# Projection of a linear-attention kernel: four fp32 tiles of 64x64 in place of three fp32r products with zero-padded weights

## The chip, the cores and the metric

The kernel runs on one core of a Trainium2 chip. The metric is the device time of one execution in microseconds (us); where several runs were made, their median. TensorE (PE in the profile) multiplies, VectorE (DVE), ScalarE (ACT) and GpSimd (POOL) work on tiles in on-chip memory (SBUF) and on the eight accumulation banks (PSUM, 2 KB per partition each), and SyncE (SP) issues nearly all transfers.

## The reference

Eight batches of eight heads of 576 tokens with 64 numbers each are put through linear attention; the result goes through a top-1 mixture of experts (MoE).

```python
def phi(x):
    proj = np.einsum('bhsd,df->bhsf', x, w_phi)                       # 64 -> 128
    proj = proj - np.max(np.abs(proj), axis=-1, keepdims=True)
    return np.concatenate([np.exp(proj), np.exp(-proj)], axis=-1)     # 256
q_p, k_p = phi(q), phi(k)
kv = np.einsum('bhsf,bhsd->bhfd', k_p, v)
z = np.sum(k_p, axis=2)
num = np.einsum('bhsf,bhfd->bhsd', q_p, kv)
den = np.einsum('bhsf,bhf->bhs', q_p, z)[..., None] + 1e-06
x = num / den        # then [4608, 512] for the experts
...
# MoE: tokens with x @ w_skip > 0 go to their best of 8 experts (512 -> 1024 -> 512)
out[do_compute] = xc + gate * (relu(xc @ w1[e]) @ w2[e])
```

The change is in the first line of phi, for q and for k.

## The kernel before

**Units and steps.** The attention works on *units*: four heads of one batch, of k or of q. There are 16 k units and 16 q units, two of each per batch. A unit has five items: item 0 is the tail (64 tokens of each head pair), items 1 to 4 are the main part (a head pair and 256 tokens each). Both streams advance by one item per step; the q stream runs 6 steps behind the k stream (`off` in CFG), so one batch of k and of q takes ten steps. Within a step the stages have lags (`lag` in CFG): load, transpose, projection one step later, exponentials at 3, use at 4, the z row at 5 and kva at 6.

**Load** (`st_load`, L251 to L259). The raw numbers of a unit lie in a tile `raw` of [128 partitions, 2 head pairs, 18 tokens, 32 numbers]; a partition is (half of the 64 numbers, head of the pair, run of 18 tokens). SP issues four DMAs per unit at L256, each to 64 partitions, 144 KB in runs of 128 bytes. Four buffers serve both streams. The load of the next unit of a stream is asked for at item 0 of the unit before it, but its buffer is free only when VectorE has made the last transpose out of it. SP works its queue in order; on it also stand the loads of v (L265, L274), the stores of `xrows` (L503, L505, L564, L566) and of `out` (L630, L635). Each DMA is bound to one of eight completion semaphores in turn, and the program makes it wait until the DMA that used that semaphore eight places earlier has landed.

**Transpose** (`st_t`, L276 to L296). VectorE transposes 32x32 blocks: the tail into `xTt` at L289, half a unit into `xT` at L291. After that a column of xT is a pair of tokens of two heads. ScalarE rounds it to fp32r (`hi`, L292), and the rest `lo` = xT - hi is made at L294, by GpSimd but for six early ones, which VectorE makes (`ini` in CFG).

**Projection** (`st_proj`, L298 to L326). Per block of 128 columns three fp32r matmuls with 256 result columns add up hi times wph, hi times wpl and lo times wph (L306 to L308). wph and wpl are the two parts of w_phi, padded with zeros so that either half of the result columns belongs to one head of the pair (`setup_w`). The result fills one PSUM bank, tag P; VectorE takes the row maximum of the absolute values (L312) and subtracts it into `u` (L321).

**Exponentials and use.** For k, ScalarE makes exp(u) and exp(-u) at L344 and L345, GpSimd sums rows for z (L353 to L359), TensorE multiplies with v (L388, L395), and z is summed in four 32-column tiles (L406). For q, TensorE transposes u into a bank U (L366), ScalarE makes the exponentials (L372, L373), TensorE multiplies with kva (L486), and VectorE divides by den in `norm` (L437 to L449). At the end of a batch `post` (L513 on) picks each token's expert on VectorE with small instructions (L538 to L561), and its stores go out through SP.

**What sets the order.** On TensorE the order of steps 8 to 78 is written out by hand; elsewhere a scheduler orders each engine's instructions by what it expects of the times, and the order is fixed before the program runs. PSUM is one pool for attention and MoE: K one bank, P three, U two, O two. The experts follow from L756 on; they load weights, round them to fp32r in parts (L188, L189) and multiply.

Of the kernel before, what the change touches and what calls it, by code (L numbers as in the profile page):

```python
# [20 lines left out]
CFG = {'ql': -2, 'q1': 0, 'vtl': 3, 'at': 6, 'cp': 0, 'ini': 'vvpvppvvpvp', 'inz': '', 'lo': {('E', 0): 'pppvpppp', ('E', 1): 'pppppppp'}, 'lod': 'vppvvvpv', 'seq': ('E', 'E', 'C', 'C', 'SC', 'D', 'DS', 'C', 'C', 'D'), 'pre': (2,), 'rows': (1, 2), 'rxg': (0,) * 6, 'lag': (1, 3, 4, 5, 6), 'post': (4, 5, 7), 'hook': (-1, -1, -1), 'man': (8, 79), 'dnow': 0, 'off': 6, 'order': 'EPAZUT', 'direct': (), 'nb': {'K': 1, 'P': 3, 'U': 2, 'O': 2}, 'apools': (('ld', 2), ('hl', 5), ('up', 5), ('zp', 2), ('ep', 7), ('kvp', 6), ('xp', 2)), 'mpools': (('rawp', 1), ('mx', 2), ('mo', 2), ('wseta', 1), ('wsetb', 1))}  # L21
# [3 lines left out]
def kernel(  # L25
# [27 lines left out]
    # a row of xrows: the token, its gate, its number  # L53
# [3 lines left out]
    # slots: full ones, ones of up to 192 tokens, ones of up to 128  # L57
# [9 lines left out]
    ps = ctx.enter_context(tc.tile_pool(name="ps", bufs=2, space=PSUM))  # L67
    NB = CFG["nb"]
    DIRECT = CFG["direct"]

    xrows = dram.tile([NTOK, XW], F32, name="xrows")

    def bank(tag):
        return ps.tile([P, 512], F32, tag=tag, name="ps_" + tag, bufs=NB[tag])
# [7 lines left out]
    # w_phi in the rows of either head of a pair, and which rows are whose  # L82
    wsrc = const.tile([P, NF], F32, name="wsrc")
    own = const.tile([P, 2], F32, name="own")
    nc.vector.memset(own, 0.0)
    for dh in range(2):
        for hd in range(2):
            nc.vector.memset(own[dh * 64 + hd * 32:dh * 64 + hd * 32 + 32, hd:hd + 1], 1.0)
    wph = const.tile([P, 2 * NF], F32R, name="wph")
    wpl = const.tile([P, 2 * NF], F32R, name="wpl")  # L90

    def setup_w():
        for hd in range(2):
            c = slice(hd * NF, (hd + 1) * NF)
            nc.scalar.activation(out=wph[:, c], in_=wsrc, func=AF.Copy, scale=own[:, hd:hd + 1])
            nc.vector.scalar_tensor_tensor(
                out=wpl[:, c], in0=wsrc, scalar=own[:, hd:hd + 1], in1=wph[:, c].bitcast(F32),
                op0=ALU.mult, op1=ALU.subtract)
# [8 lines left out]
    # the tails of a quad's v, each pair in its own rows, zeros in the other's  # L107
# [16 lines left out]
    # of every slot: the rows to gather and the rows to scatter to  # L124
# [85 lines left out]
    def places(g, pad, v):  # L210
        # v is 0 in an empty place, else 1 + the row to gather; what to add so that no row is scattered from an empty one
        nc.vector.tensor_scalar(out=g, in0=v, scalar1=-1.0, scalar2=0.0, op0=ALU.add, op1=ALU.max)
        nc.vector.tensor_scalar(out=pad, in0=v, scalar1=0.0, scalar2=BIG, op0=ALU.is_equal, op1=ALU.mult)

    early = []
    # ------------------------------------------------------------------ attention
    with ExitStack() as actx:
        pools = {}
        for nm, bufs in CFG["apools"]:
# [3 lines left out]
        # a head is 32 runs of 18 tokens; partition (half of d, head of the pair, run)  # L223
# [6 lines left out]
        # rows of xrows: two batches after each other, then the tails of both  # L230
# [8 lines left out]
        for b in range(B):  # L239
            for kind in ("k", "q"):  # L240
                for hq in range(NQ):
                    u = Unit()
                    u.kind, u.b, u.hq, u.g = kind, b, hq, b * NQ + hq
                    u.u, u.e, u.z, u.hlp = {}, {}, {}, {}
# [6 lines left out]
        def st_load(u):  # L251
            src = kv_in[u.kind]
            u.raw = ld.tile([P, 2, 18, 32], F32, tag="raw", name="raw", bufs=4)
            for pr in range(2):
                for dh in range(2):
                    nc.sync.dma_start(  # L256
                        out=u.raw[dh * 64:dh * 64 + 64, pr],
# [466 lines left out]
        for t in range(n + OFF + LA):  # L724
# [26 lines left out]
            if t == 0:  # L751
                setup_w()
# [382 lines left out]
```

## Time and profile before

| | before |
|---|---|
| time, median of 3 runs (lowest to highest) | 683.41 us (681.26 to 686.98) |
| span of the profiled execution | 681.4 us |
| attention, from the start to the last product with kva | about 390 us |
| busy: PE / DVE / ACT / POOL | 600.5 / 539.6 / 373.7 / 440.7 us |
| L306 to L308, busy | 80.8 + 73.2 + 73.4 us in 768 matmuls, which overlap |

A page of the profile lists, for each group of instructions, the source line, the engine, what is written and read, the count, the busy time with the mean duration, and after the last bar the time that the engine stood idle just before those instructions, with what ended the idle time. Busy spans of neighbouring instructions of an engine overlap a little, so sums of durations are some per cent too long. On SP the time of a row is the time that issuing took.

### The profile page before, as it was taken

What the parts mean: (1) busy time and instruction counts of PE and PEld (TensorE: products, weight loads), DVE (VectorE), ACT (ScalarE), POOL (GpSimd) and SP (SyncE); (2) the same over time, 40 slices, a digit from 0 to 9 for tenths busy, and PEclk for the clock granted to TensorE, in tenths of its full rate; (3) what the DMA queues carried; (4) which work ended last, traced back from release to release, by engine and by line L of the source; (5) the groups of instructions that cost most, each with busy time, mean ns of one, the idle gap of its engine ahead of it and who ended that gap; (6) DMA issues with size and microseconds to landing.
All of it is one profiled execution on the core that took longest, in us unless ns stands there. A gap on an engine that the chain in (4) does not pass through costs nothing. (4 is left out here: it accounts for less than half of the span.)

```text
span 681.4 us, 16258 instructions
## 1 busy us (share of the span) xinstructions
PE 600.5 (88%) x6045; PEld 514.2 (75%) x6045; DVE 539.6 (79%) x1216; ACT 373.7 (55%) x747; POOL 440.7 (65%) x383
## 2 busy tenths in 40 slices
PE   4897999979998889999899991999999989979994
PEld 3585888768877778877788881888878879868893
DVE  6868888887978978978998799679988876677830
ACT  4566665647565475656564533147757556555510
POOL 6886777777777596868774458276575485374411
PEclk9898999999999999999999996899989999999998
DMA  9898664857675667655316387269788877774500
GB/s 130 127 145 157 112 168 91 160 108 133 144 144 90 146 117 133 142 103 114 105 33 195 114 222 232 72 203 296 249 262 268 268 238 267 251 238 139 192 17 27
DMA packets 221684, 108.17 MB, mean 159 GB/s; under 512 B 160293, under 2 KB 202405, under 8 KB 221604
## 3 DMA queue, kind: packets, MB, share of 16 engines
q1 hardware_dynamic: 218272, 97.60, 58.8%
q0 software_dynamic: 3200, 9.45, 4.0%
q8 instruction: 49, 0.80, 0.5%
q14 instruction: 31, 0.25, 0.1%
q10 hardware_dynamic: 132, 0.07, 0.0%
HBM read 83.86 MB, written 24.02 MB: 158 GB/s over the span
## 5 line engine op out<-in xcount | busy, mean ns | idle before, releaser
L189 POOL TENSOR_TENSOR w<-wraw_c,w 128x1024 fp32r<-128x1024 f32 x45 | 109.9, 2454 | 70.6 <-ACT w L188 64.3
L188 ACT ACTIVATE w<-wraw_c 128x1024 fp32r<-128x1024 f32 x96 | 101.0, 1057 | 56.9 <-DMA wraw_c<-in_moe_w_dram 44.9
L353 POOL TENSOR_TENSOR z<-ek 128x512 f32<-128x512 f32 x64 | 81.7, 1277 | 54.9 <-ACT ek L345 45.1
L312 DVE TENSOR_REDUCE m<-ps_P 128x4 f32<-128x512 f32 (+1 forms) x160 | 96.4, 620 | 3.7 <-PE ps_P L308 3.6
L321 DVE TENSOR_TENSOR u<-ps_P,m 128x512 f32<-128x512 f32 (+1 forms) x160 | 95.9, 621 | 0.4
L306 PE MATMUL ps_P<-wph,hi 128*128 128x256 f32 x256 | 80.8, 316 | 16.6 <-ACT hi L292 8.5
L486 PEld LDWEIGHTS ps_O<-kva,eq 128*64 128x64 f32 x2048 | 75.2, 137 | 18.0 <-ACT eqt L373 7.3
L189 DVE TENSOR_TENSOR w<-wraw_c,w 128x1024 fp32r<-128x1024 f32 x51 | 75.4, 1481 | 14.6 <-ACT w L188 14.5
L486 PE MATMUL ps_O<-kva,eq 128*64 128x74 f32 x2048 | 78.4, 229 | 5.0 <-ACT eqt L373 3.2
L294 POOL TENSOR_TENSOR lo<-xT,hi 128x512 fp32r<-128x512 f32 x61 | 78.1, 1280 | 5.0 <-ACT hi L292 4.8
L308 PE MATMUL ps_P<-wph,lo 128*128 128x256 f32 x256 | 73.4, 287 | 0.0
L307 PE MATMUL ps_P<-wpl,hi 128*128 128x256 f32 x256 | 73.2, 286 | 0.0
L388 PE MATMUL ps_K<-ek,v 128*64 128x256 f32 x512 | 71.3, 396 | 1.5 <-DMA v<-in_v_dram 1.5
L372 ACT ACTIVATE eq<-ps_U 128x512 f32<-128x512 f32 x64 | 37.9, 593 | 57.2 <-PE ps_U L366 49.2
L306 PEld LDWEIGHTS ps_P<-wph,hi 128*128 128x128 f32 x256 | 49.4, 193 | 20.4 <-ACT hi L292 9.0
L908 PE MATMUL ps_O<-w,hh 128*128 128x512 f32 x160 | 62.4, 400 | 1.4 <-DVE hh L796 1.3
L836 POOL DMA_INDIRECT out_dram<-o,si x17 | 22.2, 1305 | 54.1 <-DVE o L834 44.4
L913 PE MATMUL ps_O<-w,hlo 128*128 128x512 f32 x120 | 49.0, 410 | 5.1 <-DVE hlo L796 5.1
L307 PEld LDWEIGHTS ps_P<-wpl,hi 128*128 128x128 f32 x256 | 49.7, 194 | 0.0
L308 PEld LDWEIGHTS ps_P<-wph,lo 128*128 128x128 f32 x256 | 49.6, 194 | 0.2 <-DVE lo L294 0.2
L366 PE MATMUL ps_U<-ident,u 128*128 128x128 f32 x288 | 48.4, 286 | 0.6 <-DVE u L321 0.6
L289 DVE STREAM_TRANSPOSE xTt<-raw 128x128 f32<-128x128 f32 x32 | 9.9, 309 | 48.8 <-DMA raw<-in_k_dram 26.8
(233 smaller groups left out, 1570.9 us busy)
## 6 DMA issues: line engine op xcount, KB each, us to landing
wraw_c<-in_moe_w_dram SPq DMA_DIRECT2D x96, 512.0 KB, 4.6
raw<-in_k_dram SPq DMA_DIRECT2D x64, 144.0 KB, 4.0
raw<-in_q_dram SPq DMA_DIRECT2D x64, 144.0 KB, 4.1
v<-in_v_dram SPq DMA_DIRECT2D x64, 128.0 KB, 3.7
out_dram<-xm SPq DMA_DIRECT2D x32, 256.0 KB, 4.4
xrows<-xm SPq DMA_DIRECT2D x8, 516.0 KB, 4.2
xrows<-xm SPq DMA_DIRECT2D x8, 512.0 KB, 4.7
vt<-in_v_dram SPq DMA_DIRECT2D x64, 16.0 KB, 2.6
```

Source lines behind the costliest of these rows:

```text
L188: nc.scalar.activation(out=hi, in_=raw, func=AF.Copy)
L189: (eng or nc.vector).tensor_tensor(out=lo, in0=raw, in1=hi.bitcast(F32), op=ALU.subtract)
L294: (nc.vector if CFG["ini"][nlo[0] - 1:nlo[0]] == "v" else nc.gpsimd).tensor_tensor(out=lo, in0=xT, in1=hi.bitcast(F32), op=ALU.subtract)
L306: nc.tensor.matmul(o, hi[:, c], wph, start=True, stop=False)
L307: nc.tensor.matmul(o, hi[:, c], wpl, start=False, stop=False)
L308: nc.tensor.matmul(o, lo[:, c], wph, start=False, stop=True)
L312: nc.vector.tensor_reduce(out=m[:, 0:nt], in_=pv, axis=AX.X, op=ALU.max, apply_absolute_value=True)
L321: nc.vector.tensor_tensor(out=uu[:, 0:nt, :], in0=pv, in1=m[:, 0:nt].rearrange("p (t o) -> p t o", o=1).broadcast_to([P, nt, NF]), op=ALU. ...
L353: zeng.tensor_tensor(out=z, in0=e[:, 0:2, :], in1=e[:, 2:4, :], op=ALU.add)
L388: nc.tensor.matmul(o[hd * 64:hd * 64 + 64, :], u.v[:, 2 * pr + hd, g * D:(g + 1) * D], u.e[i][:, 2 * j + hd, :], start=(g == 0), stop=False,)
L486: nc.tensor.matmul(ov[s * 64:s * 64 + 64, 2 * j + hd, :], e[:, half, j, hd, s * 64:s * 64 + 64], kva[:, half, 2 * pr + hd, :], start=(half ...
L908: nc.tensor.matmul(y[sub], hh[:, t], wh[:, fi, :], start=first, stop=False)
```

## The change

- `st_load`: the raw partition order becomes (head of the pair, half of the numbers, run), so that after the 32x32 transposes one head lies in the partitions 0 to 63 and the other in 64 to 127. Each unit is loaded by eight DMAs of 32 partitions and 72 KB in place of four of 64 partitions.
- `st_t`: no hi and no lo; the projection reads xT itself, which gets five buffers in place of two. 96 instructions leave ScalarE, 90 GpSimd, 6 VectorE.
- `st_proj`: per block of 128 columns four fp32 matmuls, one for each head of the pair (64 rows of the array) and each 64 tokens (64 columns), with 128 result columns each. Each head has a PSUM bank of its own, so a P tile takes two banks.
- w_phi lies once in either half of the partitions (`wp`), as it comes; wsrc, own, wph, wpl and `setup_w` go.
- PSUM: the attention has its own pool with K one, P two tiles of two banks, U one and O two; the MoE gets the former numbers in a pool that is opened after the attention.
- Paths that the settings never took (`DIRECT`, `dnow`) and comments go.

```diff
-'nb': {'K': 1, 'P': 3, 'U': 2, 'O': 2}
+'nb': {'K': 1, 'P': 2, 'U': 1, 'O': 2}, 'mb': {'K': 1, 'P': 3, 'U': 2, 'O': 2}
...
+    wp = const.tile([P, NF], F32, name="wp")
...
             for pr in range(2):
-                for dh in range(2):
-                    nc.sync.dma_start(
-                        out=u.raw[dh * 64:dh * 64 + 64, pr],
-                        in_=src[u.g, pr][:, :, dh * 32:dh * 32 + 32],
-                    )
+                for hd in range(2):
+                    for dh in range(2):
+                        r = hd * 64 + dh * 32
+                        nc.sync.dma_start(
+                            out=u.raw[r:r + 32, pr],
+                            in_=src[u.g, pr][hd * 32:hd * 32 + 32, :, dh * 32:dh * 32 + 32],
+                        )
...
-            nc.scalar.activation(out=hi, in_=xT, func=AF.Copy)
-            nlo[0] += 1
-            (nc.vector if CFG["ini"][nlo[0] - 1:nlo[0]] == "v" else nc.gpsimd).tensor_tensor(
-                out=lo, in0=xT, in1=hi.bitcast(F32), op=ALU.subtract)
-            u.hlp[(i + 1) // 2] = (hi, lo)
+            u.xT[(i + 1) // 2] = xT
...
-            p = bank("P")
+            p = ps.tile([P, 2, 512], F32, tag="P", name="ps_P", bufs=NB["P"])
...
-                nc.tensor.matmul(o, hi[:, c], wph, start=True, stop=False)
-                nc.tensor.matmul(o, hi[:, c], wpl, start=False, stop=False)
-                nc.tensor.matmul(o, lo[:, c], wph, start=False, stop=True)
+                for hd in range(2):
+                    r = slice(hd * 64, hd * 64 + 64)
+                    for sd in range(2):
+                        c = g * P + sd * 64
+                        nc.tensor.matmul(
+                            p[sd * 64:sd * 64 + 64, hd, j * NF:(j + 1) * NF], xT[r, c:c + 64], wp[r],
+                            start=True, stop=True)
...
+    psp.append((ctx.enter_context(tc.tile_pool(name="psm", bufs=2, space=PSUM, reuse_waits="tile")), CFG["mb"]))
```

Where instructions stand after the change is seen at three places. Before, a line number is that of the kernel before; after, that of the changed one (L246 is the raw load there, L277 and L279 the two transposes, L293 the projection, L299 and L301 the maximum and the subtraction, L410 to L422 the division).

**SP, one batch in the middle of the attention.** First the part with the odd unit's loads (raw from in_k_dram and from in_q_dram), before:

```order
67 L256 DMA raw<-in_k_dram 64x18x32 x4
68 L265 DMA v<-in_v_dram 32x4x256 x4
69 L274 DMA vt_91<-in_v_dram 32x2x64 x2
70 L256 DMA raw<-in_q_dram 64x18x32 x3
71 L503 DMA xrows<-xm 512x1x256
72 L256 DMA raw<-in_q_dram 64x18x32
73 L635 DMA out_dram<-xt 32x512 x4
```

and now:

```order
69 L246 DMA raw<-in_k_dram 32x18x32 x3
70 L476 DMA xrows<-xm 512x1x256
71 L246 DMA raw<-in_k_dram 32x18x32 x5
72 L246 DMA raw<-in_q_dram 32x18x32 x8
73 L264 DMA vt_79<-in_v_dram 32x2x64 x2
74 L608 DMA out_dram<-xt 32x512 x4
```

The v loads went behind the loads of q, and the `xrows` store, which stood inside the q loads, now stands inside the k loads. Then the part with the even unit's loads, before:

```order
75 L256 DMA raw<-in_k_dram 64x18x32 x4
76 L265 DMA v<-in_v_dram 32x4x256 x4
77 L274 DMA vt_90<-in_v_dram 32x2x64 x2
78 L256 DMA raw<-in_q_dram 64x18x32 x4
79 L630 DMA out_dram<-xm 32x4x512 x4
80 L274 DMA vt_91<-in_v_dram 32x2x64 x2
81 L564 DMA xrows<-xm 512x1x258
82 L566 DMA xrows<-xt 128x258
```

and now:

```order
77 L246 DMA raw<-in_k_dram 32x18x32 x8
78 L603 DMA out_dram<-xm 32x4x512 x2
79 L537 DMA xrows<-xm 512x1x258
80 L539 DMA xrows<-xt 128x258
81 L603 DMA out_dram<-xm 32x4x512 x2
82 L246 DMA raw<-in_q_dram 32x18x32 x8
```

The k and the q loads of the even unit were followed by the stores of `out` and `xrows`; now these stand between k and q.

**VectorE, the wait for the odd k unit.** The last rows up to the tail transpose of the next k unit (xTt, with the new `raw`), before:

```order
181 L441 RECIPROCAL rec_1447<-den_1446 128x4
182 L591 TENSOR_REDUCE rki_1465<-rm_1464 128x4
183 L448 TENSOR_TENSOR xm_1361<-ps_O_1429,rec_1447 128x2x128
184 L449 TENSOR_TENSOR lgm_1362<-ps_O_1429,rec_1447 128x2x18
185 L592 TENSOR_SCALAR rkp_1466<-rki_1465 128x4
186 L596 TENSOR_SCALAR RKH_99<-rki_1465 128x4
187 L312 TENSOR_REDUCE m_1501<-ps_P_1494 128x4
188 L604 SCALAR_TENSOR_TENSOR rm4_1206<-RKH_99,OH_97 128x32 x4
189 L312 TENSOR_REDUCE m_1512<-ps_P_1505 128x4
190 L321 TENSOR_TENSOR u_1503<-ps_P_1494,m_1501 128x512
191 L321 TENSOR_TENSOR u_1514<-ps_P_1505,m_1512 128x512
192 L289 STREAM_TRANSPOSE xTt_2507<-raw_2111 128x128
```

and now:

```order
191 L301 TENSOR_TENSOR u_1601<-ps_P_1590,m_1599 128x2x2x128
192 L410 TENSOR_SCALAR den_1627<-ps_O_1610 128x4
193 L414 RECIPROCAL rec_1628<-den_1627 128x4
194 L421 TENSOR_TENSOR xm_1365<-ps_O_1610,rec_1628 128x2x128
195 L422 TENSOR_TENSOR lgm_1366<-ps_O_1610,rec_1628 128x2x18
196 L299 TENSOR_REDUCE m_1659<-ps_P_1650 128x4
197 L279 STREAM_TRANSPOSE xT_2049<-raw_1377 128x4x4x32
198 L301 TENSOR_TENSOR u_1661<-ps_P_1650,m_1659 128x2x2x128
199 L299 TENSOR_REDUCE m_1672<-ps_P_1663 128x4
200 L301 TENSOR_TENSOR u_1674<-ps_P_1663,m_1672 128x2x2x128
201 L410 TENSOR_SCALAR den_1711<-ps_O_1694 128x4
202 L277 STREAM_TRANSPOSE xTt_2514<-raw_2112 128x128
```

The transpose that sets the buffer for this load free is row 174 before and row 190 now, just above the rows shown: 18 rows apart from the waiting one before, 12 now. For the other three loads of the batch these rows are 15, 12 and 14 apart before (201 to 216, 228 to 240, 245 to 259), and 17, 23 and 29 now (197 to 214, 237 to 260, 245 to 274).

**TensorE, a full step.** Before (rows of L306 to L308 repeat three more times behind these):

```order
575 L486 MATMUL ps_O<-kva,eq 64x74 x16
576 L366 MATMUL ps_U<-ident,u 128x128 x4
577 L306 MATMUL ps_P<-wph,hi 128x256
578 L307 MATMUL ps_P<-wpl,hi 128x256
579 L308 MATMUL ps_P<-wph,lo 128x256
```

and now:

```order
435 L339 MATMUL ps_U<-ident,u 128x128 x4
436 L293 MATMUL ps_P<-wp,xT 64x128 x16
437 L361 MATMUL ps_K<-ek,v 64x256 x4
438 L368 MATMUL ps_K<-ekt,vt_80 64x256 x2
439 L459 MATMUL ps_O<-kva,eq 64x74 x16
```

The step keeps its places by the order written by hand; twelve matmuls of 256 result columns became sixteen 64x64 ones of 128 result columns.

More of the change, by code (lines that the diff above doesn't have):

```diff
@@ L66 @@
     small = ctx.enter_context(tc.tile_pool(name="small", bufs=4))
-    ps = ctx.enter_context(tc.tile_pool(name="ps", bufs=2, space=PSUM))
     NB = CFG["nb"]
-    DIRECT = CFG["direct"]
     xrows = dram.tile([NTOK, XW], F32, name="xrows")
+    psp = []
     def bank(tag):
-        return ps.tile([P, 512], F32, tag=tag, name="ps_" + tag, bufs=NB[tag])
+        pool, bufs = psp[-1]
+        return pool.tile([P, 512], F32, tag=tag, name="ps_" + tag, bufs=bufs[tag])
     ident = const.tile([P, P], F32, name="ident")
@@ L218 @@
         pools = {}
+        ps = actx.enter_context(tc.tile_pool(name="ps", bufs=2, space=PSUM))
+        psp.append((ps, NB))
         for nm, bufs in CFG["apools"]:
@@ L284, in st_t @@
                 return
[L285 to L287 removed]
+            xT = hl.tile([P, n], F32, tag="xT" + sfx, name="xT" + sfx)
             if i == 0:
@@ L684 @@
         later = []
-        now, nlo, nz = [0], [0], [0]
+        now, nz = [0], [0]
         streams = []
@@ L693 @@
         streams = [(x[0], x[1], 0 if j == 0 else OFF) for j, x in enumerate(streams)]
[L694 to L697 removed]
+        for hd in range(2):
+            nc.scalar.dma_start(out=wp[hd * 64:hd * 64 + 64], in_=w_phi)
         st_load(streams[0][1][0])
```

60 lines of the change are left out of this document (10 added, 50 removed).

## The prediction, made before the result was known

> **What bounds the kernel now.** I read the busy times first, by stretches of 50 us in the middle of the attention, then VectorE's groups there, then its timeline and SP's around one batch.
>
> ```profile
> 100.00:150.00 50.00, 44.13 (x574) 36.84 (x573) 40.82 (x118) 28.85 (x70) 37.32 (x37) 1.00 0.64 130
> 150.00:200.00 50.00, 47.94 (x635) 40.51 (x637) 43.37 (x122) 32.44 (x78) 40.31 (x39) 1.00 0.61 123
> 200.00:250.00 50.00, 44.42 (x580) 37.21 (x577) 41.88 (x115) 28.63 (x68) 36.23 (x36) 1.00 0.65 131
> 250.00:300.00 50.00, 47.33 (x650) 40.19 (x649) 40.11 (x118) 30.27 (x72) 37.96 (x37) 1.00 0.65 132
> ```
>
> After the stretch come the busy times of PE, its weight loads, DVE, ACT and POOL. PE is the busiest at about 92%, DVE has 166.2 of 200 us. But the busiest need not be the one that is waited for. VectorE's groups from 100 to 300 us, with the idle time and its cause at the end:
>
> ```profile
> L312 DVE TENSOR_REDUCE m<-ps_P 128x4 f32<-128x512 f32 x69 | 45.3, 675 | 0.0
> L321 DVE TENSOR_TENSOR u<-ps_P,m 128x512 f32<-128x512 f32 x68 | 44.6, 673 | 0.0
> L312 DVE TENSOR_REDUCE m<-ps_P 128x2 f32<-128x256 f32 x17 | 6.7, 397 | 0.6 <-PE ps_P L308 0.6
> L289 DVE STREAM_TRANSPOSE xTt<-raw 128x128 f32<-128x128 f32 x18 | 5.6, 312 | 32.2 <-DMA raw<-in_k_dram 17.5 <-DMA raw<-in_q_dram 13.3 <-issue 1.5
> L550 DVE TENSOR_TENSOR oh<-key,km 128x40 f32<-128x40 f32 x2 | 2.2, 1081 | 0.0
> L551 DVE SCALAR_TENSOR_TENSOR OH<-L,oh 128x32 bf16<-128x32 f32 x2 | 1.8, 913 | 0.0
> L550 DVE TENSOR_TENSOR oh<-key,km 128x32 f32<-128x32 f32 x2 | 0.4, 187 | 0.0
> ```
>
> Of DVE's 33.8 idle us, 32.2 stand before one instruction, the tail transpose of the next unit, which waits for its raw load; DVE waited for a projection 0.6 us. So the attention runs at DVE's pace plus the refill of raw. The refill in one batch (VectorE's timeline, then SP's; the bracket is the idle time before):
>
> ```profile
> 205.05 0.31 DVE L289 STREAM_TRANSPOSE xTt<-raw 128x128 f32<-128x128 f32 x1 [2.71 <-DMA raw<-in_q_dram]
> 209.34 0.70 DVE L291 STREAM_TRANSPOSE xT<-raw 128x512 f32<-128x512 f32 x1
> 216.84 0.31 DVE L289 STREAM_TRANSPOSE xTt<-raw 128x128 f32<-128x128 f32 x1 [2.33 <-DMA raw<-in_k_dram]
> 225.13 0.31 DVE L289 STREAM_TRANSPOSE xTt<-raw 128x128 f32<-128x128 f32 x1 [0.35 <-DMA raw<-in_q_dram]
> 241.33 0.31 DVE L289 STREAM_TRANSPOSE xTt<-raw 128x128 f32<-128x128 f32 x1 [1.86 <-DMA raw<-in_k_dram]
> ```
>
> ```profile
> 199.26 0.82 SPq L503 DMA_DIRECT2D xrows<-xm  x1
> 210.07 3.45 SPq L256 DMA_DIRECT2D raw<-in_k_dram  x4
> 222.45 3.23 SPq L630 DMA_DIRECT2D out_dram<-xm  x4
> 233.09 0.57 SPq L566 DMA_DIRECT2D xrows<-xt  x1
> ```
>
> The transpose at 209.34 frees a buffer, SP issues the four DMAs from 210.07 to 213.52, and the data are there at 216.84: 3.45 us of issuing and 3.3 us more. One batch waits 2.71 + 2.33 + 0.35 + 1.86 = 7.25 us in its four refills.
>
> **The change part by part.** The sum is made against the profiled span, 681.4 us.
>
> *Work taken off ScalarE and GpSimd.* Two groups of L294 on GpSimd (of its groups in the whole run) and the larger of L292 on ScalarE go:
>
> ```profile
> L294 POOL TENSOR_TENSOR lo<-xT,hi 128x512 fp32r<-128x512 f32 x61 | 78.1, 1280 | 5.0 <-ACT hi L292 4.8
> L294 POOL TENSOR_TENSOR lot<-xTt,hit 128x128 fp32r<-128x128 f32 x29 | 13.6, 470 | 4.5 <-ACT hit L292 4.4 <-PE ps_O L406 0.2
> L292 ACT ACTIVATE hi<-xT 128x512 fp32r<-128x512 f32 x64 | 40.1, 628 | 4.5 <-DVE xT L291 3.5 <-PE ps_P L307 0.6 <-DVE den L437 0.3
> ```
>
> Both engines have room, so by itself this is worth nothing; DVE's refill is the cover. What it gives is fewer slow small instructions on DVE: L550 takes 1081 ns in one batch and 187 in another, L551 up to 913. These two rows alone lose 1.8 and 1.5 us in 200; with L542, L544 and the other shape of L551 I put the loss at 6.7. If it comes from GpSimd's work beside it, lo's share counts: 91.7 us over some 350 are 52 of the 151.8 us that GpSimd is busy in the four stretches, a third. A third of 6.7 us, over 350 us: **-4 us** (bounds 0, if the cause is another, and -7).
>
> *The projections.* TensorE's timeline:
>
> ```profile
> 206.03 0.28 PE L307 MATMUL ps_P<-wpl,hi 128*128 128x256 f32 x1
> 206.15 0.28 PE L308 MATMUL ps_P<-wph,lo 128*128 128x256 f32 x1
> 207.53 0.36 PE L306 MATMUL ps_P<-wph,hit 128*128 128x256 f32 x1 [0.75 <-DVE u L321]
> 208.97 1.20 PE L486 MATMUL ps_O<-kva,eq 128*64 128x74 f32 x32
> 210.10 0.66 PE L366 MATMUL ps_U<-ident,u 128*128 128x128 f32 x4
> 216.37 0.64 PE L406 MATMUL ps_O<-z,ones_f 128*32 128x256 f32 x8
> ```
>
> The products start 0.12 us apart, so a full step's twelve take 1.42 us. An fp32 product stands as two records (L406 has four in the program, eight in the row). No row of before has 64-row tiles. If four tiles run together as the four of L406 do, 32 records go at L486's pace (32 in 1.13 us, 35 ns each) or a little faster: 0.9 to 1.1 us. If only two run together, 35 ns times 128/74 gives 61 ns, 1.94 us. I take the first, since L406 is the nearest row in tile count. TensorE gains 0.3 to 0.5 us of some 4.1 per step (92% of the 4.4 that a step takes, below). DVE is not waiting for it, so in the middle this is worth nothing; the cover is gone behind 300 us, where loads end and DVE does wait for PE: 4.5 us from 310 to 390 (quoted next). There **-3 us** (bounds 0 and -5).
>
> ```profile
> 310.00:390.00 80.00, 76.64 (x1061) 63.87 (x1058) 70.61 (x222) 47.89 (x107) 51.80 (x47) 1.00 0.39 111
> L312 DVE TENSOR_REDUCE m<-ps_P 128x4 f32<-128x512 f32 (+1 forms) x30 | 18.6, 632 | 2.8 <-PE ps_P L308 2.7
> L437 DVE TENSOR_SCALAR den<-ps_O 128x4 f32<-128x4 f32 x20 | 3.0, 152 | 2.0 <-PE ps_O L486 1.8
> ```
>
> A rule speaks against the tiles. The Trainium skill, "TensorEngine Tiling (Array Packing)", section "Key Properties", says that changing the tiling mode drains TensorE; a step would change twice more. Its trace here: L366 to L306 in one mode and L388 in another differ by 0.08 us at each change, 0.16 us per step, which TensorE's gain covers either way.
>
> *The raw loads.* Eight DMAs of half the size replace four, and three blocks move on SP. Prices:
>
> ```profile
> L256 SPq DMA_DIRECT2D raw<-in_k_dram x64: 539/764/2527, 0.8 to 281.2; - x64
> DMA to landing us min/median/max: 2.9/4.1/5.9
> L274 SPq DMA_DIRECT2D vt<-in_v_dram x64: 311/425/1056, 16.0 to 330.9; - x64
> vt<-in_v_dram SPq DMA_DIRECT2D x64, 16.0 KB, 2.6
> L289 DVE STREAM_TRANSPOSE xTt<-raw 128x128 f32<-128x128 f32 x32 | 9.9, 309 | 48.8 <-DMA raw<-in_k_dram 26.8
> ```
>
> (Issue time in ns, minimum, median, maximum; landing in us; the third and fourth row are the small v tails, from their line and the DMA table, the last is the page's own for L289 in the whole run.) Issuing a 32-partition load lies between the vt median, 0.43 us, and the median of the larger raw load, 0.76; I take 0.50, about midway between vt and the cheapest raw load, 0.54. Landing lies between 2.6 and 4.1; I take the 3.3 of the refill above, since a unit's bytes stay the same. DVE's work from the order's rows with the durations above:
>
> - Odd k: SP does 8 x 0.50, and in the middle of it the `xrows` store, 0.82: 4.8 + 3.3 = 8.1 us. DVE has 4.9 us of work from row 190 to 202. Wait 3.2.
> - Odd q, right behind it: 4.8 + 4.0 + 3.3 = 12.1 us from k's release. DVE reaches row 214 after 4.9 + 3.2 + 4.3 = 12.4. Wait 0.
> - Even k: 4.0 + 3.3 = 7.3 us, DVE has over 8 (rows 237 to 260). Wait 0.
> - Even q: SP stands at the `xrows` store until row 256 of DVE (its data, L534); behind it are q's loads. Then 2 x 0.57 + 2 x 0.8 for stores, 4.0, 3.3: 10.0 us. DVE has 7.2 us left to row 274. Wait 2.8.
>
> That is 6.0 us per batch against 7.25. 18 tail transposes in 200 us, four to a batch, make 44 us a batch (7.25 us in each would be 32.6 in 200, and the row has 32.2). From about 50 us, when buffers are first reused, to the last load, issued near 305, that is some 5.5 batches: **-7 us**. With 0.43 and 2.6 the same sums give 1.9 + 0 + 0 + 1.6, -21 us; with 0.76 and 4.1 they give 6.0 + 1.8 + 1.2 + 4.5 = 13.5, +34 us. The Trainium skill, "DMA: Bandwidth & Descriptors", section "Anatomy of one DMA", puts a fixed cost of about 2 us on each DMA, mostly the receipt of its completion; vt's 16 KB in 2.6 us against raw's 144 KB in 4.1 agree. By it halving a DMA would save some 0.7 us of landing, and the wait of odd k would be 2.5, not 3.2.
>
> *PSUM.* P goes from three tiles to two, U from two banks to one. The row at 207.53 shows what a late tile costs TensorE (0.75 us for u at L321). DVE frees a P tile with each pair of L312 and L321, so TensorE can be one projection ahead, not two. Bounds: nothing, and 0.2 us per step, 16 us in 80 steps. I take 0.05, **+4 us**, because DVE now waits 0.6 us per 200 for P, so slack is there.
>
> *Start and transition.* Six lo's leave VectorE's first 25 us, and hi and lo leave the first unit's chain, while the first transpose waits for four issues, not two:
>
> ```profile
> 8.52 0.69 DVE L294 TENSOR_TENSOR lo<-xT,hi 128x512 fp32r<-128x512 f32 x1 [0.20 <-ACT hi L292]
> 0.79 8.87 SPq L256 DMA_DIRECT2D raw<-in_k_dram  x8
> PE ps_K L1020 <- DVE rx L1015: 11.7, 1, 11.7
> ```
>
> **-3 us** (+2 to -4). At the end of the attention the MoE's banks are a new pool, so its first products start behind the last product with kva; but TensorE stands idle 11.7 us there anyway (last row, TensorE's waits from 380 to 440 us). **+2 us** (-2 to +5).
>
> The sum: 681.4 - 4 - 3 - 7 + 4 - 3 + 2 = 670.4. The median of the runs shown, 683.41, lies 2.0 above the profiled span, so the forecast is **672 us**, faster by 1.7%. About 1% is what a measurement of this kernel can tell from no change, from 676.6 to 690.2 us.
>
> **The rivals.**
>
> *No change, 688 us.* Issuing takes 0.6 us (4.0 + 0.5 + 0 + 3.6 = 8.1 per batch, +5 us), and with two P tiles DVE waits 0.1 us in each of 80 steps, +8. With the other terms 681.4 - 10 + 2 + 13 + 2.0 = 688.4. Half-concurrent tiles lead there too: 1.94 in place of 1.42 us makes TensorE's step 4.6 us, a little over the present 4.4. For it: the median issue of 0.76; PE at 92%. Against it: vt at 0.43.
>
> *Slower, 710 us: the refill queue.* At 0.76 us per issue, 16 loads back to back need 12 us, and with eight completion semaphores only 8 x 72 KB can be on their way, half of before, so a long landing (4.1) holds up issuing too. +34 in place of -7: 681.4 + 34 - 10 + 2 + 2.0 = 709.4 (a late load covers the P term). It decides from the point where eight issues and the landing exceed 8 us. Against it: a refill of four took 6.8 us for the same bytes.
>
> *Slower, 695 us: two P tiles.* If VectorE waits 0.33 us in each step, 26 us: 681.4 - 7 - 10 + 2 + 26 + 2.0 = 694.4. For it: TensorE is late by 0.75 us in the step of 207.53 already with three. Against it: DVE's 0.6 us.
>
> **How the numbers follow.** The forecast has 0.46, no change 0.28, the refill queue 0.14, the P tiles 0.12; so faster by over 1% is 0.46, within 1% 0.28, slower 0.26. The low end is the sum with the cheap loads (-21): 656, and a little more from the other bounds, 652. The high end takes in no change and the P tiles, 698; beyond it lies most of the refill queue, and little below. The forecast's own range is 652 to 676.
>
> **What would show it.** Right: L277's idle time below 45 us (48.8 before, whole run), most of it at odd k and even q; L246 near 0.5 us an issue; L293 with 32 records in about 1.1 us; DVE's wait at L299 for PE near 4 us; POOL 92 and ACT 50 us less. The forecast fails if L246 costs over 0.65 us or its waits pass 60 us, if DVE waits over 12 us at L299, or if L293 takes more than 1.5 us per step.

## The result, and the profile after

The changed kernel takes 757.49 us (median of 4 runs, 756.03 to 759.10), the kernel before 685.19 us in the same comparison: a ratio of 1.105 (95% interval 1.1005 to 1.1104), 10.5% slower. The prediction was 672 us, in a range of 652 to 698.

The part that changed is the attention. The last product with kva (L486 before, L459 after) starts at 389.6 us before and at 450.6 after; what follows it takes 291.8 us of the span before and 304.3 after. So 61 of the 73.5 us are lost inside the attention, 12.5 where it ends.

The same four stretches of the changed kernel as were shown of before (busy PE, weight loads, DVE, ACT, POOL, then the granted clock):

```profile
100.00:150.00 50.00, 40.67 (x677) 30.84 (x675) 35.85 (x101) 20.79 (x48) 22.27 (x21) 0.86 0.51 109
150.00:200.00 50.00, 37.76 (x650) 27.87 (x648) 33.35 (x97) 20.47 (x48) 21.15 (x21) 0.90 0.55 114
200.00:250.00 50.00, 40.08 (x645) 30.47 (x640) 33.40 (x102) 18.80 (x46) 19.84 (x19) 0.84 0.56 112
250.00:300.00 50.00, 39.77 (x664) 29.55 (x662) 34.15 (x96) 23.28 (x54) 23.31 (x22) 0.88 0.52 109
```

Every one of these engines is idler than before: DVE has 136.7 of 200 us where it had 166.2. None of them became the bound; all of them wait. Only SP's queue is fuller: its rows in these 200 us add up to 143 us, 120 before. VectorE's groups from 100 to 300 us say what it waits for:

```profile
L299 DVE TENSOR_REDUCE m<-ps_P 128x4 f32<-128x512 f32 x57 | 38.6, 678 | 4.6 <-PE ps_P L293 4.6
L277 DVE STREAM_TRANSPOSE xTt<-raw 128x128 f32<-128x128 f32 x15 | 4.7, 312 | 54.1 <-DMA vt<-in_v_dram 32.2 <-DMA raw<-in_q_dram 11.0 <-DMA raw<-in_k_dram 8.7
L410 DVE TENSOR_SCALAR den<-ps_O 128x4 f32<-128x4 f32 x32 | 4.6, 144 | 2.1 <-PE ps_O L438 1.3 <-PE ps_O L459 0.8
```

15 tail transposes in place of 18 fit into 200 us: 53.3 us a batch, not 44.4. Each batch now waits 14.4 us for raw, in place of 7.2; in the whole run it is 94.8 us in place of 48.8. The wait named after vt is one for raw too: the eight loads and vt share semaphores, and the name is that of the DMA which came last on them. One batch, first VectorE's row that frees the buffer for the q loads, its four tail transposes and the row ahead of the longest wait, then SP's rows around that wait:

```profile
203.95 0.70 DVE L279 STREAM_TRANSPOSE xT<-raw 128x512 f32<-128x512 f32 x1
209.41 0.31 DVE L277 STREAM_TRANSPOSE xTt<-raw 128x128 f32<-128x128 f32 x1 [1.77 <-DMA raw<-in_k_dram]
214.81 1.01 DVE L301 TENSOR_TENSOR u<-ps_P,m 128x512 f32<-128x512 f32 x2
222.59 0.31 DVE L277 STREAM_TRANSPOSE xTt<-raw 128x128 f32<-128x128 f32 x1 [6.77 <-DMA vt<-in_v_dram]
241.44 0.31 DVE L277 STREAM_TRANSPOSE xTt<-raw 128x128 f32<-128x128 f32 x1 [4.16 <-DMA raw<-in_q_dram]
246.73 0.31 DVE L277 STREAM_TRANSPOSE xTt<-raw 128x128 f32<-128x128 f32 x1 [1.44 <-DMA vt<-in_v_dram]
```

```profile
201.33 5.92 SPq L246 DMA_DIRECT2D raw<-in_k_dram  x8
207.35 1.04 SPq L603 DMA_DIRECT2D out_dram<-xm  x2
208.50 0.75 SPq L537 DMA_DIRECT2D xrows<-xm  x1
209.30 2.68 SPq L603 DMA_DIRECT2D out_dram<-xm  x2
212.08 1.12 SPq L478 DMA_DIRECT2D xrows<-xt  x1
213.24 6.61 SPq L246 DMA_DIRECT2D raw<-in_q_dram  x8
```

The buffer for the q loads is free at 204.65 us, but on SP k's loads stand ahead of them until 207.25 and the stores until 213.20. So SP comes to the q loads at 213.24, issues them until 219.85, and the transpose starts 2.74 us later. VectorE was done at 215.8 with all that stands before the tail transpose in its order, and everything behind it waited 6.77 us. Four loads took 3.45 us to issue before; eight half as large take 5.3 to 6.6 (one issue in ns: least, median and most):

```profile
L246 SPq DMA_DIRECT2D raw<-in_k_dram x128: 566/630/1970, 0.8 to 351.6; - x128
```

### The profile page after: what moved, and what is told of

Read it like the earlier page. It is cut to its first block, busy times and chain, and to the rows that moved or that the text cites. A ratio compares the mean times of both kernels' runs of the same rounds, so it can differ in the third digit from the quotient of the medians.

```text
span 754.9 us, 19224 instructions
## 1 busy us (share of the span) xinstructions
PE 609.6 (81%) x7485; PEld 492.2 (65%) x7485; DVE 539.7 (71%) x1203; ACT 335.7 (44%) x649; POOL 357.9 (47%) x293
## 5 line engine op out<-in xcount | busy, mean ns | idle before, releaser
L293 PE MATMUL ps_P<-wp,xT 64*64 64x128 f32 x2048 | 88.3, 302 | 42.2 <-DVE u L301 28.3
L299 DVE TENSOR_REDUCE m<-ps_P 128x4 f32<-128x512 f32 (+1 forms) x160 | 99.1, 624 | 14.6 <-PE ps_P L293 14.5
L459 PEld LDWEIGHTS ps_O<-kva,eq 128*64 128x64 f32 x2048 | 82.9, 150 | 34.6 <-DVE rm L562 19.4
L293 PEld LDWEIGHTS ps_P<-wp,xT 64*64 64x64 f32 x2048 | 64.8, 147 | 60.4 <-issue 37.4
L459 PE MATMUL ps_O<-kva,eq 128*64 128x74 f32 x2048 | 87.0, 243 | 17.1 <-DVE rm L562 17.1
L301 DVE TENSOR_TENSOR u<-ps_P,m 128x512 f32<-128x512 f32 (+1 forms) x160 | 98.1, 620 | 2.1
L175 DVE TENSOR_TENSOR w<-wraw_c,w 128x1024 fp32r<-128x1024 f32 x51 | 76.0, 1498 | 13.7 <-ACT w L174 13.5
L361 PE MATMUL ps_K<-ek,v 128*64 128x256 f32 x512 | 77.6, 426 | 0.4 <-DMA v<-in_v_dram 0.4
L277 DVE STREAM_TRANSPOSE xTt<-raw 128x128 f32<-128x128 f32 x32 | 9.9, 311 | 94.8 <-DMA vt<-in_v_dram 41.6
L317 ACT ACTIVATE ek<-u 128x512 f32<-128x512 f32 x64 | 40.4, 631 | 61.9 <-DVE u L301 61.9
L878 PE MATMUL ps_O<-w,hh 128*128 128x512 f32 x160 | 63.5, 401 | 0.9 <-DVE hh L766 0.6
L567 POOL TENSOR_SCALAR OP<-iota_p,rkp 128x128 bf16<-128x128 f32 x31 | 18.2, 602 | 67.9 <-DVE RKH L569 67.9
L361 PEld LDWEIGHTS ps_K<-ek,v 128*64 128x64 f32 x512 | 34.6, 147 | 23.9 <-issue 14.7
L279 DVE STREAM_TRANSPOSE xT<-raw 128x512 f32<-128x512 f32 x64 | 44.6, 699 | 5.4 <-DMA raw<-in_q_dram 3.2
L882 PE MATMUL ps_O<-w,hh 128*128 128x512 f32 x120 | 48.4, 405 | 0.0
```

What stands on the lines that cost most here:

```text
L175: (eng or nc.vector).tensor_tensor(out=lo, in0=raw, in1=hi.bitcast(F32), op=ALU.subtract)
L293: nc.tensor.matmul(p[sd * 64:sd * 64 + 64, hd, j * NF:(j + 1) * NF], xT[r, c:c + 64], wp[r], start=True, stop=True)
L299: nc.vector.tensor_reduce(out=m[:, :, 0:n], in_=pv, axis=AX.X, op=ALU.max, apply_absolute_value=True)
L301: nc.vector.tensor_tensor(out=uu[:, 0:nt, :].rearrange("p (t h) f -> p h t f", h=2), in0=pv, in1=m[:, :, 0:n].rearrange("p h (t o) -> p h ...
L361: nc.tensor.matmul(o[hd * 64:hd * 64 + 64, :], u.v[:, 2 * pr + hd, g * D:(g + 1) * D], u.e[i][:, 2 * j + hd, :], start=(g == 0), stop=False,)
L459: nc.tensor.matmul(ov[s * 64:s * 64 + 64, 2 * j + hd, :], e[:, half, j, hd, s * 64:s * 64 + 64], kva[:, half, 2 * pr + hd, :], start=(half ...
```

## The experiments

Theory A was that the raw refill costs the time (twice as many issues on SP), B that two P tiles and one U bank do, C that the second PSUM pool delays the experts, D that the order of the work, which the scheduler made anew for the tiles, does. Theory E came later: of that order it is the place of one instruction on VectorE's queue, the tail transpose. The table has each kernel's time, the start of its last product with kva, the rest of the profiled span behind that, and the idle time before the tail transpose in the whole run.

| kernel | time, us (kernel before beside it) | last kva product | rest | idle before xTt |
|---|---|---|---|---|
| before | | 389.6 | 291.8 | 48.8 |
| changed | 757.5 (685.2) | 450.6 | 304.3 | 94.8 |
| e1 changed, four loads | experts not comparable | 430.7 | | 74.3 |
| e2 before, eight loads | 712.9 (680.5) | 418.7 | 294.8 | 61.9 |
| e3 before, P 2 and U 1 | 706.6 (680.5) | 390.3 | 313.0 | 34.0 |
| e6 before, two pools | 693.5 (680.5) | 386.0 | 304.9 | 42.1 |
| e9 before, all but the tiles | 725.3 (686.6) | 415.9 | 310.4 | 57.0 |
| e4 changed, six raw buffers | 703.6 (686.6) | 401.1 | 304.4 | 46.5 |
| e5 before, five raw buffers | 685.6 (686.6) | 391.3 | 293.4 | 50.0 |
| e7 changed, q loads by ScalarE | 713.2 (686.6) | 405.2 | 305.6 | 50.4 |
| e11 changed, two xTt | 680.5 (686.7) | 377.3 | 302.8 | 7.4 |
| e10 changed, two xT and xTt | 700.0 (686.7) | 392.0 | 306.3 | 15.8 |
| e8 changed, DVE order by hand | 762.3 (686.7) | 457.0 | 305.5 | 6.1 |
| e12 before, DVE order by hand | 1014.2 (686.7) | 717.7 | 294.8 | 0.3 |
| e14 before, two tail hi and lo | 672.6 (686.6) | 375.9 | 293.6 | 11.1 |
| e16 e11 with one pool | 711.0 (686.6) | 373.1 | 338.2 | 8.5 |
| e15 e11 with four loads | experts not comparable | 361.5 | | 5.0 |
| e19 e11, q loads by ScalarE | 671.9 (681.0) | 363.5 | 306.3 | 4.0 |
| e20 e11, half of all loads by ScalarE | 667.7 (681.0) | 361.5 | 300.8 | 5.6 |

**One part alone, or undone.** e1 takes the four loads back into the changed kernel, where the numbers then lie in the wrong partitions, so that only its attention's time is read; e2 does the reverse in the kernel before, in its own partition order (`r = dh * 64 + hd * 32`):

```diff
-                for hd in range(2):
-                    for dh in range(2):
-                        r = hd * 64 + dh * 32
-                        nc.sync.dma_start(
-                            out=u.raw[r:r + 32, pr],
-                            in_=src[u.g, pr][hd * 32:hd * 32 + 32, :, dh * 32:dh * 32 + 32],
-                        )
+                for dh in range(2):
+                    nc.sync.dma_start(
+                        out=u.raw[dh * 64:dh * 64 + 64, pr],
+                        in_=src[u.g, pr][:, :, dh * 32:dh * 32 + 32],
+                    )
```

> The changed kernel with the four 64-partition raw loads of before (144 KB each) in place of the eight; the numbers then lie in the partitions of the old order, so the projections mix the heads' halves and only the time is read. Theory A (the refill of raw: an issue costs nearly the same for half the size, so eight issues hold SP twice as long): the idle time before the tail transpose falls from 94.8 to about 50 us and the time from 757 to 710-720 us. Theory B (two P tiles and one U bank let TensorE and VectorE wait for each other): the idle time before the tail transpose falls little, to no less than 85 us, and the time stays above 740 us.

> The kernel before with eight 32-partition raw loads (72 KB) per unit, nothing else changed. Theory A: the idle time before the tail transpose rises from 48.8 to 85-95 us, time 715-730 us. Theory B: within 1% of before, 678-692 us.

In e1 the last product with kva came 19.9 us earlier than in the changed kernel, and 74.3 us of the wait for raw stayed where about 50 were expected; in e2 it came 29.1 us later than in the kernel before, and the whole took 32 us more (ratio 1.045, 1.032 to 1.059), with 61.9 us of wait where 85 to 95 were expected. So the eight loads cost 20 to 30 us of the attention's 61, and A is true but not enough.

e3 is `'nb': {'K': 1, 'P': 2, 'U': 1, 'O': 2}` in the kernel before; e6 gives its experts a pool of their own (`psp.append(ctx.enter_context(tc.tile_pool(name="psm", ...)))` behind the attention).

> The kernel before with two P banks and one U bank in place of three and two, nothing else. Theory A: within 1.5% of before, 680-695 us, VectorE waits for P under 10 us. Theory B: 720 us or more, VectorE's wait for P over 30 us.

> The kernel before with PSUM in two pools, one for the attention and one opened after it for the experts, with the old numbers of banks. Theory C (the end of the attention: the experts' first products come 12 us after the last product with kva in the changed kernel, at once in the kernel before): 692-699 us. If the new pool is not what delays them: 681-689 us.

e3 came out between, at 706.6 us, and the table shows why its total misleads: its attention ends at 390.3 us, 0.7 later than before. The 21 us are lost behind it, since in the kernel before the experts draw on the same banks; the changed kernel gives them their old numbers back. So B falls for the attention. e6 loses 13 us behind the last product with kva, as much as the changed kernel does: C holds. TensorE's rows there:

```profile
386.12 1.10 PE L777 MATMUL ps_U<-ident,xg 128*128 128x128 f32 x8
387.05 0.18 PE L582 MATMUL ps_O<-Stot,ones_b 128*128 128x40 bf16 x1
390.77 0.19 PE L585 MATMUL ps_O<-OH,tri 128*128 128x40 bf16 x1 [3.54 <-DVE OH L553]
393.75 1.09 PE L777 MATMUL ps_U<-ident,xg 128*128 128x128 f32 x4 [1.44 <-issue]
```

With a new pool the experts' transposes (L777) come behind the attention and the last batch's ranks (L582, L585) ahead of the first expert products; in the kernel before these run at once.

e9 joins all of it in the kernel before but keeps hi, lo and the three products:

> The kernel before with all of the change but the projection itself: eight raw loads, PSUM in two pools, in the attention two P banks and one U bank, in the experts the old numbers; three fp32r products with hi and lo stay. If the parts add up (eight loads +29 us to the last product with kva, P and U +1, the new pool +13), 725 us and a last product with kva at 420 us. If the tiles and the missing hi and lo cost nothing of their own, it is as slow as the changed kernel, 750-760 us and 451 us: then loads and PSUM hurt each other.

The parts add up: 725.3 us, and 415.9 for the last product with kva (420 expected). The tiles, with the buffers that came with them, cost the remaining 35 us of the attention, though they take work away. That pointed to the order of the work, which is made anew for each kernel.

**More buffers, another queue.** In e4 and e5 the line is `tag="raw", name="raw", bufs=6` and `bufs=5`; in e7 the loads of q use `nc.scalar.dma_start`.

> The changed kernel with six raw buffers in place of four, so that loads can start a unit earlier; it issues as many DMAs. Theory A (the loss in the attention is the latency of the raw refill): the idle time before the tail transpose falls from 94.8 to under 20 us, the last product with kva comes at 385 us or earlier (450.6 in the changed kernel) and the time is 690 us or less. Theory D (the order of VectorE's and TensorE's work, which the scheduler set otherwise for the tiles, makes them wait for each other): the waits move to the projections and the time stays above 720 us.

> The kernel before with five raw buffers (six do not fit). If the refill of raw bounds its attention too, the idle time before the tail transpose falls from 48.8 to under 25 us and the time by 10 to 25 us, to 655-670 us. If TensorE, 92% busy, is then the bound, by less than 5 us.

> The changed kernel with the q loads issued by ScalarE's queue in place of SP's; the same DMAs. Theory A: q no longer stands behind k and the stores, its waits fall by more than half, 715-730 us, unless ScalarE's own work is held up by the waits for free buffers. Theory D: above 740 us.

e4 wins 49 us of the attention, but 46.5 us of wait remain, so that it fits neither expectation; e7 wins 45. e5 gives nothing (ratio 0.998, 0.994 to 1.001): with one buffer more, the kernel before waits as long as with four. In its order the scheduler used the buffer to put the transposes earlier: VectorE's work between a release and the next tail transpose into that buffer is 4.2 to 6.5 us in the middle of its attention, 4.5 to 6.2 in the kernel before. This gave theory E.

**The place of the tail transpose.** e11 changes one number; e10 has `bufs=2` for both transposes:

```diff
-            xT = hl.tile([P, n], F32, tag="xT" + sfx, name="xT" + sfx)
+            xT = hl.tile([P, n], F32, tag="xT" + sfx, name="xT" + sfx, bufs=2 if i == 0 else 5)
```

The rows of VectorE's order that release a buffer and that wait for the load into it, first in the changed kernel, then in e11:

```
245 L279 STREAM_TRANSPOSE xT_2453<-raw_1802 128x4x4x32
274 L277 STREAM_TRANSPOSE xTt_3012<-raw_2602 128x128
...
243 L279 STREAM_TRANSPOSE xT_2453<-raw_1802 128x4x4x32
319 L277 STREAM_TRANSPOSE xTt_3012<-raw_2602 128x128
```

> The changed kernel with two buffers for the tail's transpose (xTt) in place of five; nothing else. By its order VectorE now has about 25 us of work between the transpose that frees a raw buffer and the next tail transpose into it, in place of 4.5 to 9. Theory E (the loss in the attention is the place of the tail transpose on VectorE's queue, which five xTt buffers allow far ahead of its use, so that the queue stands until the load has landed): the idle time before the tail transpose falls from 94.8 to under 15 us, the last product with kva comes at 395 us or earlier (450.6), 690 to 705 us, although the eight loads stay. Theory A in its strict form (eight issues hold SP for too long whatever VectorE does): above 725 us.

> The changed kernel with two buffers each for xT and xTt. By its order VectorE has 9 to 12 us between release and tail transpose. Theory E: between the changed kernel and the version with two xTt alone, 700 to 725 us. Theory A, strict: above 725 us.

e11 takes 680.5 us: 77 us come back by this one number, and the kernel is 0.9% faster than before (ratio 0.991, 0.987 to 0.995) with its eight loads, its PSUM and its late experts. The idle time before the tail transpose is 7.4 us. VectorE's groups of e11 in the whole run and of e10:

```profile
L277 DVE STREAM_TRANSPOSE xTt<-raw 128x128 f32<-128x128 f32 x32 | 9.7, 305 | 7.4 <-DMA raw<-in_q_dram 4.6 <-DMA raw<-in_k_dram 2.8
```

```profile
L277 DVE STREAM_TRANSPOSE xTt<-raw 128x128 f32<-128x128 f32 x32 | 9.9, 308 | 15.8 <-DMA raw<-in_q_dram 7.3 <-DMA raw<-in_k_dram 5.0 <-DMA v<-in_v_dram 2.4
```

e10, with 9 to 13 us between release and use, lies between, as expected. E stands as a cure, and A in its strict form falls. The scheduler moved other rows too; what ties the gain to the tail transpose is that the idle time before it fell by 87 us.

E doesn't say why the changed kernel lost against the one before. VectorE's work between the release and the tail transpose is 5.3, 4.5, 6.2 and 5.3 us for the four loads of a batch before (205 to 242 us) and 6.3, 9.3, 4.8 and 5.9 us now (209 to 247 us): on the whole the transposes stand later than before, not earlier. The refill grew by more than this work did. e9 has 27 to 30 us of such work in a batch, the changed kernel 26, so the place of the transpose explains at most a part of the 35 us between these two, and the rest is open. One rival is that the `xrows` and `out` stores now stand between k's and q's loads on SP; no run moves them.

e8 and e12 take VectorE's order from the scheduler altogether: `manual_schedule(engines={mybir.EngineType.PE, mybir.EngineType.DVE})`.

> The changed kernel with VectorE's order of steps 8 to 78 as the program is written, as TensorE's already is; the tail transpose then stands just ahead of its use, some 25 us of VectorE's work behind the release. Theory E: idle before the tail transpose under 15 us, last product with kva by 400 us, 690 to 710 us; waits for P may grow, since the small expert instructions then stand in one block. Theory A, strict: above 725 us.

> The kernel before with VectorE's order of steps 8 to 78 as written. Theory E for the kernel before too: the 48.8 us of idle time before its tail transpose fall under 15 us; what of it is gained depends on TensorE, 92% busy: 665 to 690 us.

Both lose the wait for raw, as E says, and both are far slower than expected: less wait there is not less time. The transposes now stand too late. TensorE's waits from 40 to 400 us, of e8 and then of e12:

```profile
PE ps_P L293 <- DVE xT L279: 61.4, 39, 4.6
```

```profile
PE ps_P L306 <- ACT hi L292: 66.0, 30, 4.7
PE ps_P L308 <- POOL lo L294: 40.2, 30, 4.3
```

A transpose directly ahead of its projection leaves no time for the projection, and in the kernel before none for hi and lo.

**The same cure for the kernel before.** e14 gives the tail's hi and lo two buffers (`bufs=2 if i == 0 else 5`); its xTt has two.

> The kernel before with two buffers in place of five for the tail's hi and lo (its xTt has two already); by its order VectorE then has 10 to 17 us between release and tail transpose, in place of 4.4 to 6.1. Theory E for the kernel before: its 48.8 us of idle time before the tail transpose fall under 15 us; TensorE, at 92%, becomes the bound, so that half or less of it is gained: 660 to 676 us. If the wait of before has another cause: no change, 680 to 690 us.

672.6 us, ratio 0.981 (0.978 to 0.984). The wait falls from 48.8 to 11.1 us, 13.7 us of it are gained in the attention. The bound that was read from the profile, the refill, was itself a matter of order.

**What the loads still cost.** e16 is e11 with the two pools made one (experts draw halves of the P tiles); e15 is e11 with e1's loads.

> The changed kernel with two buffers for xTt and one PSUM pool for attention and experts: the experts take halves of the two-bank P tiles (four banks) and one U bank. Theory C: the experts' first products come right behind the last product with kva again, 13 us less than with xTt alone (680.5): 664 to 672 us. If fewer U banks or the shared halves hold up the experts by as much: 676 to 685 us.

> The changed kernel with two buffers for xTt and the four 64-partition raw loads of before; the numbers lie in the wrong partitions, so tokens go to other experts and only the attention's time is read. If the eight loads still cost something once VectorE has 25 us between release and use: the last product with kva comes 5 us or more earlier than at 377.3 us. If they are hidden then: within 3 us of 377.

e16 slows the experts to 338 us, so it cannot show C in the changed kernel; only e6 does. e15 ends its attention 15.8 us before e11: eight loads still cost that. The times of SP's rows in e11 add up to 193.4 of the 200 us from 100 to 300 (166.3 in e15): SP hardly stood idle there. VectorE of e11 waits for the `xrows` stores on that queue, too (7.2 us in all, in four waits; 0.5 us in e15, nothing in e20):

```profile
DVE xm L421 <- DMA xrows<-xm: 7.2, 4, 3.7
```

e19 and e20 move half of the raw issues to ScalarE's queue (`(nc.sync if u.kind == "k" else nc.scalar).dma_start`, and `hd == 0` for the kind):

> The changed kernel with two buffers for xTt and the q loads on ScalarE's queue. The four-load version with the same two buffers (numbers misplaced) ended its attention at 361.5 us, the eight-load one at 377.3. If those 16 us are SP's issuing: half the raw issues on another queue bring the last product with kva to 362 to 369 us and the time to 664 to 673 us, below the kernel before with its tail buffers cut (672.6). If they come from the DMAs themselves (eight small ones landing later): no earlier than 374 us, 677 us or more.

> As the one with the q loads on ScalarE's queue, but four of the eight loads of every unit, of k and of q, go there (those of the second head of a pair). The first unit's load is split too, so the start is shorter; ScalarE issues as many. If SP's issuing is what costs: 362 to 368 us for the last product with kva, 662 to 672 us; if not, 677 us or more.

The last product with kva comes at 363.5 and 361.5 us, as with four loads: it was the issuing, not the smaller DMAs. With 667.7 us e20 is 1.8% faster than the kernel before (0.982, 0.976 to 0.989), the best with the tiles; e14, without them, has 0.981 in another comparison, so which of the two is faster is open. VectorE's stretch of e20 from 100 to 300 us is 93% busy (third number):

```profile
100.00:300.00 200.00, 191.08 (x3580) 146.62 (x3572) 186.76 (x529) 111.84 (x264) 112.99 (x102) 1.00 0.73 147
```

## Why the prediction was wrong

*What bounds the kernel* was read rightly: VectorE, and its waits for raw; TensorE at 92% was not waited for. But the wait was taken as a property of the loads. It depended as much on where the waiting instruction stood.

*The raw loads* were the step that failed: "-7 us", from an issue price of 0.50 us and waits of 6.0 us per batch. The waits of the batch shown were 1.77 + 6.77 + 4.16 + 1.44 = 14.1 us, and in the whole run they grew by 46 us (94.8 against 48.8). An issue of half the size costs nearly as much: 566 ns at the least and 630 in the median, against 539 and 764 for the whole one, and in the bursts that VectorE waits for it was 0.66 to 0.83 us (5.3 to 6.6 us for eight). The largest wait, at even q, was put at 2.8 us and was 6.77: its loads took 6.61 us to issue in place of 4.0, and the stores ahead of them 0.75 + 1.12 + 2.68 = 4.55 us in place of 2.74. At even k VectorE had 6.3 us of work, not over 8.

The upper bound of the same sum, at 0.76 us, had given 13.5, which is partly luck: it has a landing of 4.1 us where 3.0 was the median, and waits of 6.0 us at odd k and 4.5 at even q. The way of adding up held; its prices were too low. The slower rival, the refill queue at 710 us, was the nearest, though not by its longer landing. It got 0.14, set against a refill of four that took 6.8 us; the price of 0.50 leaned on vt, and a DMA of 64 runs was no guide to one of 576. The low end, 656 us, lacks the 2.0 us between span and time that the other sums have.

*xT's five buffers* had no term at all. The change part quoted rows 12 to 29 apart between release and use, and the sum used them as given. That two numbers, the distance and the number of xTt buffers, hang together was not asked; e11 shows that the buffers alone are worth 77 us, e9 that without the tiles and their buffers the loss is 39 of 72. But five buffers were no new thing: the tail's hi and lo had as many before, and e14 shows what two of them win there.

*PSUM*, +4 us, was too much for the attention of the kernel before (e3: 0.7). In the changed kernel VectorE waited 14.5 us for P, over the 12 that the prediction named as a sign of its failing, and 10.1 for den (3.6 and 1.8 before). These waits do not go with those for raw; for P, in the changed kernel, e11 and e20 (us in all, times, longest):

```profile
DVE m L299 <- PE ps_P L293: 14.5, 19, 4.8
DVE m L299 <- PE ps_P L293: 23.5, 20, 5.7
DVE m L299 <- PE ps_P L293: 13.4, 26, 5.2
```

The rival with two P tiles put 26 us on this wait, and it grew by 11. No run gives the tiles more P banks, so what the two cost there is open.

*The transition*, +2 us with the cover of 11.7 us of idle TensorE, measured 12.5. The cover was the wrong one: those waits stand later, at L1020, and are paid again (14.7 us in the changed kernel).

*The start*, -3 us, was a loss: the first product with kva came at 46.5 us, 40.4 before. Two units' loads held SP for 10.95 us in place of 8.87, but e1 and e3, with four loads, have 48.1 and 47.7, so the cause is open.

*Right* was the tiles' own price, and in its direction that of the small instructions. A full step's 32 records take 1.04 us where nothing interrupts them (the first row here to the second, TensorE in e20), against 1.42 for the twelve fp32r products; the step gains 0.4, as put. Whether this won the 3 us at the end of the attention is not shown.

```profile
201.92 1.10 PE L293 MATMUL ps_P<-wp,xT 64*64 64x128 f32 x32
202.96 0.64 PE L379 MATMUL ps_O<-z,ones_f 128*32 128x256 f32 x8
```

VectorE's small instructions are no longer slow; before, in the whole run, and after:

```profile
L550 DVE TENSOR_TENSOR oh<-key,km 128x40 f32<-128x40 f32 x4 | 3.4, 838 | 0.0
L542 DVE TENSOR_TENSOR d<-L,mx 128x40 f32<-128x40 f32 x4 | 3.3, 816 | 0.0
```

```profile
L523 DVE TENSOR_TENSOR oh<-key,km 128x40 f32<-128x40 f32 x4 | 0.8, 200 | 0.0
L515 DVE TENSOR_TENSOR d<-L,mx 128x40 f32<-128x40 f32 x4 | 0.8, 191 | 0.0
```

These two alone give 5.1 us, where 4 were put down for all. Their cause is open: most kernels without hi and lo show about 190 to 200 ns (e8 has 762 for the first), those with them anything from 201 (e12) to 1388 (e3), and no run took only GpSimd's lo away.

So the change does make the attention shorter: with the tail transpose late and the issues on two queues it ends 14 us earlier than e14's (361.5 against 375.9); so does e15's, with four loads on SP as in e14. As made, it lost 61 us, most of them to the wait for raw, which the longer refill nearly doubled and which a later tail transpose takes away.

## What to carry to other kernels

A wait that dominates an in-order engine has two sides: how long the transfer takes, and how early the waiting instruction stands in the queue. Count the work between the instruction that frees a buffer and the one that waits for its refill; if the output of the waiting one has more buffers than it needs, a scheduler may put it far ahead, and fewer buffers can be faster (e11, e14; in e10, where xT lost buffers too, less so). When a transfer is split, count issues, not bytes, and take the price of an issue from a row with a like number of runs.

## What the runs showed of the hardware

A raw load's issue on SP takes at least 566 ns for 576 runs of 128 bytes and 539 ns for 1152, so its floor is no lower for half the size; a v tail of 64 runs takes at least 311. In e11 SP's rows fill 193 of 200 us, and half of the raw issues on ScalarE's queue brought the last product with kva 14 to 16 us forward. Landing fell only from 4.0 to 3.0 us for half the bytes.

Stalls went with a slower clock. The granted clock of TensorE is 1.00 from 100 to 300 us before and 0.84 to 0.90 after. Behind idle time the same instruction was slower (some of TensorE's rows of the changed kernel where the experts begin):

```profile
460.27 0.19 PE L556 MATMUL ps_O<-OH,tri 128*128 128x40 bf16 x1 [8.45 <-DVE OH L524]
463.13 1.09 PE L744 MATMUL ps_U<-ident,xg 128*128 128x128 f32 x4 [1.32 <-issue]
464.44 0.41 PE L852 MATMUL ps_P<-x,w 128*128 128x256 f32 x1
464.66 0.41 PE L851 MATMUL ps_P<-x,w 128*128 128x256 f32 x1
466.35 0.28 PE L851 MATMUL ps_P<-x,w 128*128 128x256 f32 x1
466.47 0.28 PE L852 MATMUL ps_P<-x,w 128*128 128x256 f32 x1
```

After 8.45 idle us the products start 0.22 us apart, from 466.35 on 0.12. The 3.54 idle us of e6 above had the same effect (0.21 us apart from 394.85 to 399.54), the 1.54 us at 394.44 in the kernel before had none. The Trainium skill, "TensorE: Matmul & The Clock Gate", Part 1, says that the array falls to half its clock after an idle window of about 3.4 us and comes back after as long a busy one. These rows agree roughly: the products are fast 3.2 us after the last gap ends at 463.13. How much of the 61 us this took is open: no run holds the clock fixed.
